# Two weight sums moved in VectorE's queue, four state copies given to ScalarE, one unit's scores moved up: a blocked attention followed by a bilinear feed-forward

## The chip, the cores and the metric

The kernel runs on one core of one Trainium2 chip. The metric is the time of one launch in device microseconds, as the median of several executions. A profile of one execution is at hand for each kernel. Engines in the profile: PE is TensorE's matmuls, PEld its weight loads, DVE is VectorE, ACT is ScalarE, POOL is GpSimd, SP is SyncE, which here issues transfers.

## The reference, cut to what matters

```python
# attention: 4 batches, 8 heads, 768 positions, 64 per head
intra = (qb @ kb^T * Dmask) @ vb             # within a block, decay lam^(i-j), lower triangle
inter = (qb * lam_pow) @ kv_state            # from the blocks before
out[block] = intra + inter
kv_state = lam_block * kv_state + (kb * rev_pow)^T @ vb
# feed-forward on x = attention output, 3072 x 512
a = x @ w_a ; b = x @ w_b                    # 512 x 1536 each
out = (a * b) @ w_out                        # 1536 x 512
```

## The kernel before

The work is cut into 24 units of 128 positions (six units make one sequence of a batch), and the units into seven groups. While TensorE does the feed-forward of one group, hooks at numbered slots insert the attention of later units. What goes where is a table, `PLAN`:

```python
ACT_COPY = (14, 16, 17, 18, 20, 21)          # units whose state copy is ScalarE's
FIRST_COPY = (15, 19)
PLAN = {
    0: [...(9, "P", 4), (9, "TW", 4), (9, "L", ...), (11, "P", 5), ...,
        (14, "T", 4), (17, "S", 4), (17, "P", 6), ..., (21, "V", 4), (22, "S", 5), (22, "LS", 9), ...,
        (29, "KS", 8), (30, "QS", 9), (33, "KS", 9), (33, "TW", 5)],
    1: [(0, "V", 6), (1, "S", 7), ...],
    2: [..., (11, "S", 10), (11, "S", 11), ..., (18, "S", 14), (19, "S", 15)],
    ...
```

P, KS and QS scale a unit's k and q by powers of lam. T transposes them on TensorE (later units are transposed by a transfer). S makes the scores of a unit and masks them. V adds to the state. L and LS issue loads. TW makes one of six *weight sums*. These serve the groups from the second on, whose feed-forward uses a scheme with seven products in place of eight and needs sums of weight blocks beforehand (the code is cut and simplified):

```python
def block_sums(t, b11, b21, b12, b22):       # four passes over 128 x 512 bf16
    nc.vector.tensor_sub(t[:, 0], b12, b11)
    nc.vector.tensor_sub(t[:, 1], b22, t[:, 0])
    nc.vector.tensor_sub(t[:, 2], b22, b12)
    nc.vector.tensor_sub(t[:, 3], b21, t[:, 1])

def piece_S(u):
    masks(u, scores(u))                      # scores: PSUM kq (TensorE); masks: m = kq * lotri (VectorE)

def kv_copy(u, ps, eng="dve"):               # state from PSUM to SBUF, its two diagonal blocks
    if eng == "act":
        for b in range(2):                   # two half copies
            nc.scalar.copy(st[p, :, b, :], ps[p, :, b, :])
    else:
        nc.vector.tensor_mul(st, ps, bdiag_bc)
```

The kernel uses seven PSUM banks in rotation. A matmul that needs a bank waits until its last reader is done (in the trace before, m_p waits 1.14 us for VectorE's mask). In the feed-forward of a group, m_q, m_r and m_p are the banks of the seven products; `c` and `ab` are sums and products made of them; `op` is the output product.

## Time and profile before

| | before |
|---|---|
| time, median of its first five runs | 220.97 us |
| span of the profiled run | 218.9 us |
| TensorE busy | 210.6 us, 96% |
| VectorE busy | 173.6 us, 79% |
| ScalarE busy | 106.8 us, 49% |

TensorE is nearly always busy, so the reading begins with its few waits and asks what stood in the other engine's queue at that moment. The prediction below shows those lines.

### The profile page before, as it was taken

The page shows a single profiled execution, that of the slowest core. Times are in us where ns is not written, and L with a number is a line of the kernel's source. Part 1 is how long each engine was busy: PE and PEld are TensorE (multiplying, and loading weights), DVE is VectorE, ACT ScalarE, POOL GpSimd, SP SyncE. Part 2 cuts the span into 40 slices and gives each one's busy share as a digit, 9 for nine tenths or more (in the row PEclk, how much of TensorE's full clock was granted, in tenths as well). Part 3 has the DMA queues.
Part 4 walks back from the last instruction along what each step waited for, and adds up shares of the span by engine and source line. Part 5 has one row for each costly group of instructions (what it writes and reads, how often), then busy time and mean ns, then how long its engine had stood idle before and what let it go on. Part 6 is the DMA issues. An engine that isn't in the chain of part 4 may idle for free.

```text
span 218.9 us, 5702 instructions
## 1 busy us (share of the span) xinstructions
PE 210.6 (96%) x2300; PEld 159.8 (73%) x2311; DVE 173.6 (79%) x309; ACT 106.8 (49%) x191; POOL 126.5 (58%) x143
## 2 busy tenths in 40 slices
PE   7799999999799999999999999999999999999994
PEld 2476444556787688865588887888987888989973
DVE  0992998956979488799968899879899787996860
ACT  3586223246771565613375636365546566443522
POOL 6879559974387279994079930599920156300330
PEclk9999999999999999999999999999999999999999
DMA  4999999999698959999999990399920500001302
GB/s 133 294 181 195 203 231 212 228 221 169 127 173 93 157 88 147 159 230 308 225 260 165 174 166 4 107 208 140 113 15 3 191 0 3 0 3 68 128 3 96
DMA packets 84686, 30.78 MB, mean 141 GB/s; under 512 B 71988, under 2 KB 81076, under 8 KB 84660
## 3 DMA queue, kind: packets, MB, share of 16 engines
q1 hardware_dynamic: 51668, 19.86, 45.2%
q0 software_dynamic: 32704, 10.49, 42.7%
q8 instruction: 18, 0.29, 0.5%
q10 hardware_dynamic: 288, 0.07, 0.1%
q14 instruction: 8, 0.07, 0.1%
HBM read 28.32 MB, written 6.29 MB: 158 GB/s over the span
## 4 chain that ended last, share of the span: by engine, by line
PE 56%; POOL 18%; DMA 13%; issue 5%; DVE 4%; SPq 2%; ACT 1%; POOLq 0%; DVEq 0%
PE m_q L565 18%; PE m_r L565 8%; PE op L802 7%; PE o_q L676 7%; POOL qk L277 5%; DMA wo_sb<-in_moe_w_out_dram 5%; PE m_p L565 4%; PE o_r L676 4%; POOL ab L612 4%; DMA kf<-in_k_dram 4%; PE o_ps L380 3%; POOL vb L299 3%; DMA k<-in_k_dram 3%; DMA qkf<-in_k_dram 2%; PE o_p L676 2%
## 5 line engine op out<-in xcount | busy, mean ns | idle before, releaser
L612 POOL TENSOR_TENSOR ab<-c,c 128x512 bf16<-128x512 bf16 x30 | 34.8, 1168 | 35.7 <-DVE c L610 35.4
L565 PEld LDWEIGHTS <-tw 128*128 128x128 bf16 x576 | 49.1, 98 | 6.1 <-issue 0.4
L565 PE MATMUL m_q<-xs,tw 128*128 128x256 bf16 (+1 forms) x288 | 36.1, 255 | 0.0
L802 PE MATMUL op<-wo_sb,ab 128*128 128x512 bf16 (+2 forms) x159 | 33.2, 347 | 0.7 <-issue 0.3
L361 DVE TENSOR_TENSOR m<-kq,lotri 128x512 bf16<-128x512 f32 x47 | 29.3, 680 | 0.1
L565 PEld LDWEIGHTS <-wa_sb 128*128 128x128 bf16 x288 | 24.7, 98 | 4.0 <-issue 1.3
L580 ACT COPY s<-m_q 128x512 f32<-128x512 f32 x30 | 17.6, 588 | 17.6 <-PE m_q L565 16.2
L619 DVE TENSOR_TENSOR ab<-c,m_q 128x512 bf16<-128x512 f32 x30 | 20.6, 686 | 6.7 <-PE m_q L565 4.4
L602 POOL TENSOR_TENSOR c<-s 128x512 bf16<-128x512 f32 x7 | 8.9, 1271 | 26.7 <-ACT s L580 26.7
L610 DVE TENSOR_TENSOR c<-u,m_r 128x512 f32<-128x512 f32 x30 | 20.4, 680 | 4.8 <-ACT u L580 4.8
L802 PEld LDWEIGHTS <-ab 128*128 128x128 bf16 x168 | 14.4, 98 | 12.3
L299 POOL DMA_DIRECT2D vb<-in_v_dram x24 | 22.3, 933 | 1.4 <-DMA wo_sb<-in_moe_w_out_dram 1.2
L599 DVE TENSOR_TENSOR c<-s,m_p 128x512 bf16<-128x512 f32 x23 | 15.8, 688 | 7.7 <-PE m_p L565 7.6
L616 DVE TENSOR_TENSOR c<-s,m_q 128x512 f32<-128x512 f32 x30 | 20.6, 685 | 0.5
L580 ACT COPY u<-m_q 128x512 f32<-128x512 f32 x30 | 17.8, 593 | 6.4 <-PE m_q L565 6.0
L580 ACT COPY s<-m_r 128x512 f32<-128x512 f32 x30 | 17.7, 590 | 6.4 <-PE m_r L565 6.4
L277 POOL TENSOR_TENSOR qk<-qf,lp_q 128x512 bf16<-128x512 f32 x18 | 18.8, 1044 | 1.2 <-DMA qf<-in_q_dram 1.2
L565 PE MATMUL m_p<-xT,wa_sb 128*128 128x256 bf16 (+1 forms) x144 | 18.1, 255 | 1.1 <-DVE m L361 1.1
L565 PE MATMUL m_q<-xT,tw 128*128 128x256 bf16 (+1 forms) x144 | 18.1, 255 | 0.3 <-DVE c L616 0.3
L403 ACT CAST xT<-o_ps 128x512 bf16<-128x512 f32 x22 | 11.9, 589 | 12.9 <-PE o_ps L380 12.5
L565 PE MATMUL m_q<-xT,wa_sb 128*128 128x256 bf16 (+1 forms) x144 | 18.1, 255 | 0.0
L565 PE MATMUL m_r<-xs,tw 128*128 128x256 bf16 (+1 forms) x144 | 18.1, 255 | 0.0
(118 smaller groups left out, 359.3 us busy)
## 6 DMA issues: line engine op xcount, KB each, us to landing
qf<-in_q_dram SPq DMA_DIRECT2D x14, 256.0 KB, 4.9
kf<-in_k_dram SPq DMA_DIRECT2D x14, 256.0 KB, 5.1
vb<-in_v_dram POOLq DMA_DIRECT2D x24, 128.0 KB, 5.5
out_dram<-o_two SPq DMA_DIRECT2D x6, 512.0 KB, 3.1
wa_sb<-in_moe_w_a_dram POOLq DMA_DIRECT2D x6, 256.0 KB, 6.2
wb_sb<-in_moe_w_b_dram POOLq DMA_DIRECT2D x6, 256.0 KB, 7.7
wo_sb<-in_moe_w_out_dram POOLq DMA_DIRECT2D x6, 256.0 KB, 8.1
out_dram<-o_kept SPq DMA_DIRECT2D x6, 256.0 KB, 5.5
```

Of the source, the lines that this page charges most:

```text
L277: eng_of(eng).tensor_mul(dst.rearrange("p (c b) d -> p b c d", b=2), x[:].rearrange("p (b c) d -> p b c d", b=2), lp.rearrange("p (b c) o ...
L299: nc.gpsimd.dma_start(out=vb, in_=vr[b, nb])
L361: nc.vector.tensor_mul(m, kq[i], lotri_bc)
L565: nc.tensor.matmul(ps[:, f, :], lhsT=w(k, f), rhs=x[:, k, :], start=(first and f == 0 and k == 0), stop=True, skip_group_check=True)
L580: nc.scalar.copy(t, ps)
L599: nc.vector.tensor_add(d["c11"], d["s12"][:, 0], p)
L610: nc.vector.tensor_add(c12, d["u2"], d["r"])
L612: nc.gpsimd.tensor_mul(ab[:, nf * i:nf * i + nf, 0:h], d["c11"], c12)
L616: nc.vector.tensor_add(d["c22"], d["s5"], d["q"])
L619: nc.vector.tensor_mul(ab[:, nf * i:nf * i + nf, h:2 * h], d["c22"], d["q"])
L676: nc.tensor.matmul(ps[:, t, :], lhsT=x(j, c)[:, t * BLK:(t + 1) * BLK], rhs=w(j)[:, c, :], start=(first and t == 0 and j == js[0] and c == ...
L802: nc.tensor.matmul(op[:, lo:hi], lhsT=ab[:, f, t * 128:(t + 1) * 128], rhs=wo_sb[:, f, lo:hi], start=(f == 0), stop=(f == FC - 1))
```

## The change

The intent: put the last two weight sums where VectorE is idle for a transfer, and take state copies off VectorE. The diff, cut to its lines:

```diff
-ACT_COPY = (14, 16, 17, 18, 20, 21)
-FIRST_COPY = (15, 19)
+ACT_COPY = (4, 10, 12, 13, 14, 16, 17, 18, 20, 21)
+FIRST_COPY = (11, 15, 19)
 ...
-        (9, "P", 4), (9, "TW", 4), (9, "L", ...
+        (9, "P", 4), (9, "L", ...
-        ... (22, "S", 5), (22, "LS", 9), (23, "P", 7), ...
+        ... (22, "S", 5), (22, "LS", 9), (22, "TW", 4), (23, "P", 7), ...
-        (30, "QS", 9), (33, "KS", 9), (33, "TW", 5)],
+        (30, "QS", 9), (31, "TW", 5), (33, "KS", 9)],
 ...
-    2: [..., (11, "S", 10), (11, "S", 11), ...
+    2: [..., (10, "S", 10), (11, "S", 11), ...
```

## The prediction

> **What bounds the kernel now.** I read the engine table first, then the list of who waited for whom on TensorE, then the order of time of TensorE and VectorE around each wait.
>
> ```profile
> PE 210.6 (96%) x2300; PEld 159.8 (73%) x2311; DVE 173.6 (79%) x309; ACT 106.8 (49%) x191; POOL 126.5 (58%) x143
> ...
> PEclk9999999999999999999999999999999999999999
> ```
>
> TensorE is busy in 210.6 of 218.9 us, at a granted clock that never drops. The change adds or removes no matmul, so it can only win part of the remaining 8.3 us. By five-microsecond stretches, 2.6 us of that gap lie in the first fifteen microseconds (1.26 + 1.01 + 0.36) and 3.15 us after 215 us (3.9 less 0.75 busy), under the last output; neither is touched. What is left is small and named by the list of waits:
>
> ```profile
> PE idle L213 <- DVE idle_sb L208: 1.3, 1, 1.3
> PE m_p L565 <- DVE m L361: 1.1, 1, 1.1
> ...
> PE kq L344 <- DVE ab L515: 0.3, 1, 0.3
> ...
> PE m_q L565 <- DVE c L616: 0.3, 1, 0.3
> ```
>
> Columns: who waited for whom, total us, times, longest. The first is the start-up. The other three all wait for VectorE, once each, and the change works exactly there. In order of time, TensorE (start, duration, work, idle before) around the three:
>
> ```profile
> 41.49 0.23 PE L344 MATMUL kq<-qkT 64*128 64x128 bf16 x1
> 42.04 0.38 PE L344 MATMUL kq<-qkT 64*128 64x128 bf16 x7 [0.32 <-DVE ab L515]
> 42.35 0.60 PE L802 MATMUL op<-wo_sb,ab 128*128 128x512 bf16 x2
> ...
> 57.82 0.61 PE L565 MATMUL m_r<-xs,tw 128*128 128x128 bf16 x8
> 59.57 0.61 PE L565 MATMUL m_p<-xT,wa_sb 128*128 128x128 bf16 x8 [1.14 <-DVE m L361]
> ...
> 60.46 0.61 PE L322 MATMUL tps<-ident,qk 128*128 128x128 bf16 x8
> 61.36 0.61 PE L565 MATMUL m_q<-xT,tw 128*128 128x128 bf16 x8 [0.29 <-DVE c L616]
> ```
>
> The reader should compare starts, not the idle figures[...]. An undisturbed set of eight scores takes 0.33 us from its start to the next (45.29 to 45.62 in the same view), a set of eight 128-column matmuls 0.45 (53.59 to 54.04), eight transposes 0.45 (42.79 to 43.24). So the three stalls cost 42.35 - 41.49 - 0.33 = 0.53 us, 59.57 - 57.82 - 0.45 = 1.30 us and 61.36 - 60.46 - 0.45 = 0.45 us. Sum: 2.28 us. That is the whole prize in reach.
>
> VectorE in the same stretch shows why:
>
> ```profile
> 37.51 1.82 DVE L277 TENSOR_TENSOR qk<-kf,lp_k 128x512 bf16<-128x512 f32 x1
> 39.25 0.41 DVE L518 TENSOR_TENSOR tw<-wb_sb,wa_sb 128x512 bf16<-128x512 bf16 x1
> ...
> 40.71 1.27 DVE L515 TENSOR_TENSOR ab<-a_sb,b_ps 128x512 bf16<-128x512 bf16 x2
> ...
> 55.10 0.69 DVE L277 TENSOR_TENSOR qk<-qkf,lp_k 128x512 bf16<-128x512 f32 x1 [2.28 <-DMA qkf<-in_k_dram]
> 55.71 0.42 DVE L518 TENSOR_TENSOR tw<-wb_sb,wa_sb 128x512 bf16<-128x512 bf16 x1
> 56.16 1.49 DVE L519 TENSOR_TENSOR tw<-wb_sb,tw 128x512 bf16<-128x512 bf16 x1
> ...
> 58.24 0.68 DVE L444 TENSOR_TENSOR st<-kvd,bdiag 128x512 bf16<-128x512 f32 x1
> 58.84 1.27 DVE L361 TENSOR_TENSOR m<-kq,lotri 128x512 bf16<-128x512 f32 x2
> ```
>
> Weight sum 4 sits ahead of the two products (ab) that free the banks the scores of unit 4 want. Weight sum 5 sits behind unit 9's k, which lands only at 55.10, and ahead of unit 7's masks; VectorE idles 2.28 us and then does the sums when TensorE needs the masks. From 76 us to 214 us the stretches leave TensorE idle for some 0.3 us in all, so nothing else of size is to be won.
>
> [...] the idle 2.28 us at 55.10 was not filled with the sums standing next in the queue. So position in program order is what the change buys. [...] eight transposes being shown as 0.61 us while the next work starts after 0.45, hence the starts above. [...] one weight-sum piece took 1.49 us instead of 0.42 while GpSimd ran a sum from 56.10 to 57.36, and k of unit 4 took 1.82 instead of 0.69 beside GpSimd's work from 37.69. [...] This is the main uncertainty for the new places of the sums.
>
> **The change part by part.** *Weight sum 4.* Its four pieces take from 39.25 to 40.71, 1.46 us. Without them the ab products, whose PSUM input is ready (no wait is shown before them), run at about 39.25 to 40.45, before the scores at 41.49: the 0.53 us go. In its new place, behind unit 5's masks, VectorE idles 2.00 us before unit 7's k, which waits for a transfer until 49.01. Masks of unit 5 ended at 47.01; with TensorE 0.53 us ahead and the state copy of unit 4 gone from the queue (0.60 us from start to start) they end near 46.4, so the sums fill 46.4 to 47.9. GpSimd's next scaling starts at 47.88; a collision would cost up to its 1.04 us, giving 48.9, still at the transfer's landing. Cost: 0 to 0.1 us.
>
> *Weight sum 5.* VectorE finishes unit 8's k at 52.8 and idles to 55.10. The sums take 1.46 us, to about 54.3; GpSimd's scaling of unit 9's q at 54.13 (1.04 us) may hold the last piece to 55.2. Then unit 9's k to 55.8, unit 6's state copy (it stays on VectorE) to 56.4, the first mask of unit 7 to 57.0, the second to 57.6. TensorE, 0.53 us ahead, wants the first bank at 57.82 + 0.45 - 0.53 = 57.74: no wait, 1.30 us go. The two sums behind the masks, 0.60 us each, end near 58.8; TensorE reaches the matmuls that waited for the second at 57.74 + 3 x 0.45 = 59.1: the 0.45 us go too, with 0.3 us to spare.
>
> *State copies of units 4, 10, 12, 13.* On VectorE one takes 0.68 us; on ScalarE it is two instructions of half the partitions:
>
> ```profile
> L442 ACT CAST st<-kvd x10: 364/367/370, 126.8 to 168.4; 64x256 bf16<-64x256 f32 x10
> ```
>
> ```profile
> L444 DVE TENSOR_TENSOR st<-kvd,bdiag x13: 677/682/692, 15.5 to 191.2; 128x512 bf16<-128x512 f32 x13
> ```
>
> That is 2 x 0.367 = 0.73 us each, 2.9 us in all on ScalarE, which is 49% busy, against 4 x 0.60 = 2.4 us of queue time off VectorE. ScalarE idles from 92.2 to 96.9 where unit 10's copy falls (its matmuls are at 93.41, its readers at 97.32), and between its output copies for 12 and 13. TensorE has no wait on VectorE there, so these three are worth 0 to 0.1 us. Unit 11 is the last block of its sequence and has no copy, so listing it with those copied first does nothing; the instruction order of the changed kernel confirms that.
>
> *Scores of unit 10 one place earlier.* TensorE's order changes only here. Its two masks (1.2 us) come before a c11 sum instead of after the last c22. That queue has about 0.45 us free in each period of 3.06 us, so the last c22 slips from 93.97 to about 94.7, against 94.94 where TensorE uses it: about 0.2 us to spare. Worth 0, with a small risk.
>
> Sum: 0.53 + 1.30 + 0.45 = 2.28, less an allowance of 0.1 to 0.2 for collisions: about 2.1 us, 1.0%. From 220.97 this gives 218.85 us.
>
> **The rivals.** *Transfers set the pace.* k of units 7 and 9 land at absolute times, and the loads of unit 10 were issued at 56.33 and 56.81, with a median landing of about 5 us; GpSimd would want them at 62.3 instead of 64.55. They land about 61.3 to 62.6, so GpSimd may wait some tenths, but it then has 1.13 us idle before its next product. Against it also: the transposes of units 8 and 9 have over 1 us of room. If it held, little of the 1.75 us after 57 us would survive: 220.2 to 220.6. [...] unit 7's or 9's k late: 0.3 to 1 us of the gain gone, 219.2 to 219.8. For it: the two collisions seen before; against it: 0.8 us of room at the first mask. *A new wait around 90 to 98 us* through unit 10's masks or ScalarE's copies: 0.2 to 0.6 us back, 219.1 to 219.5. Against it: ScalarE's idle there and the still free TensorE.
>
> **Range and chances.** The best case is 220.8 (the fastest run) less 2.3, or 218.5, less a tenth or two of luck; the likely spoilers leave 219.8. One of three runs before was 222.75, 0.8% off, so the medians can move a few tenths: range 218.1 to 219.9. Over 2% faster would need 4.4 us, more than all TensorE stalls between 15 and 214 us: 2%. Slower by over 2% would need a new chain of stalls of 4.4 us: 1%. Within 2%: 97%.
>
> **What would show it.** In the changed profile TensorE should be busy as before (210 us) with a span near 216.8; the waits on ab, m and c should be gone from its list or below 0.1; on VectorE the weight sums should stand in the former idle times before 49 and before 55 us, with those idle times down to about half a microsecond; the 70 us after 76 us should be a shifted copy. I am wrong if a wait of TensorE on VectorE of some 0.3 us or more remains between 50 and 62 us, if a wait appears at 90 to 98 us, or if the span falls by less than 1.5 us.

## The result, and the profile after

The changed kernel took 218.86 us (median of 5 runs, 218.78 to 219.09) against 220.97 (220.80 to 222.75). The ratio is 0.9889, with a 95% interval of 0.9851 to 0.9927. Ratios here are the mean time of one kernel's fast runs over that of the other's in the same rounds, so not quite the ratio of the medians.

The waits of TensorE after (who waited for whom, total us, times, longest); what is left besides these is 0.4, 0.3 and 0.2 us at the start and in gaps without a cause shown:

```profile
PE idle L213 <- DVE idle_sb L208: 1.3, 1, 1.3
PE tq L871 <- DVE scratch L864: 0.8, 3, 0.4
```

The three waits are gone. TensorE in order of time at the same three places (start, duration, work, count):

```profile
41.48 0.40 PE L344 MATMUL kq<-qkT 64*128 64x128 bf16 x8
41.81 0.60 PE L802 MATMUL op<-wo_sb,ab 128*128 128x512 bf16 x2
...
57.27 0.61 PE L565 MATMUL m_r<-xs,tw 128*128 128x128 bf16 x8
57.72 0.61 PE L565 MATMUL m_p<-xT,wa_sb 128*128 128x128 bf16 x8
...
58.62 0.61 PE L322 MATMUL tps<-ident,qk 128*128 128x128 bf16 x8
59.10 0.61 PE L565 MATMUL m_q<-xT,tw 128*128 128x128 bf16 x8
```

Each next start follows after 0.33, 0.45 and 0.48 us. Against the same instructions before, TensorE is ahead by 42.35 - 41.81 = 0.54 us at the first, 59.57 - 57.72 = 1.85 us at the second, and 61.36 - 59.10 = 2.26 us at the third.

VectorE shows how (the last bracket is the idle time before an instruction and what ended it):

```profile
46.38 0.42 DVE L518 TENSOR_TENSOR tw<-wb_sb,wa_sb 128x512 bf16<-128x512 bf16 x1
...
49.25 0.69 DVE L277 TENSOR_TENSOR qk<-kf,lp_k 128x512 bf16<-128x512 f32 x1 [1.33 <-DMA kf<-in_k_dram]
...
52.93 0.42 DVE L518 TENSOR_TENSOR tw<-wb_sb,wa_sb 128x512 bf16<-128x512 bf16 x1
...
55.36 0.69 DVE L277 TENSOR_TENSOR qk<-qkf,lp_k 128x512 bf16<-128x512 f32 x1 [0.89 <-DMA qkf<-in_k_dram]
55.97 0.68 DVE L444 TENSOR_TENSOR st<-kvd,bdiag 128x512 bf16<-128x512 f32 x1
56.57 1.28 DVE L361 TENSOR_TENSOR m<-kq,lotri 128x512 bf16<-128x512 f32 x2
```

Both sums now stand in front of a transfer that VectorE has to wait for anyway; their pieces take 0.42 to 0.43 us each, so none was held up beside GpSimd's work. The idle times that remain are 1.33 and 0.89 us. In sum TensorE's busy time is nearly as before (210.2 of 217.1 us), VectorE's is 169.9 us (3.7 less) and ScalarE's 109.4 (2.6 more).

The lead does not stay at 2.26. It falls twice. The first place is the scores of units 10 and 11 (kq). Before, in one stretch of TensorE:

```profile
92.33 0.60 PE L565 MATMUL m_q<-xs,tw 128*128 128x256 bf16 x4
92.86 0.62 PE L344 MATMUL kq<-qkT 64*128 64x128 bf16 x16
93.41 0.40 PE L411 MATMUL kvd<-vb,qk 128*128 128x128 bf16 x4
```

and after, where unit 10 has moved:

```profile
87.45 0.60 PE L565 MATMUL m_q<-xs,tw 128*128 128x256 bf16 x4
87.98 0.40 PE L344 MATMUL kq<-qkT 64*128 64x128 bf16 x8
88.31 0.61 PE L565 MATMUL m_r<-xs,tw 128*128 128x256 bf16 x4
```

Four matmuls of 256 columns take 0.44 us from their start to the next where they stand among their own kind (88.76 to 89.20 for m_p in the same view), but 0.53 us where scores of tile 64\*128 follow (92.33 to 92.86): 0.09 us are lost on the way in. Sixteen scores together take 0.55 us (92.86 to 93.41) and eight 0.33 (87.98 to 88.31), so eight more cost 0.22, and by this difference 0.11 us are a fixed part of each set. The split pays both once more: 0.09 + 0.33 + 0.33 - 0.55 = 0.20 us. (64\*128 and the like is the tile that the profile shows with a matmul.) In the trace before, sixteen scores take the same 0.55 us where matmuls of tile 64\*64 follow (96.77 to 97.32). In that trace the new weights are loaded only together with the first matmul of the new tile: the loads start at 92.86, after 0.21 us without one, and at 97.32, and so do the matmuls. Where the tile stays the same, the first load for the m_q at 92.33 starts at 92.22, 0.11 us before it. From the m_q at 89.71 (before) and 87.45 (after), a lead of 2.26, it falls to 93.41 - 91.37 = 2.04 us at the state's matmuls.

The second place is ScalarE at the start of the fifth group. Before:

```profile
141.80 0.62 ACT L580 COPY s<-m_p 128x512 f32<-128x512 f32 x1
142.28 0.63 ACT L580 COPY u<-m_q 128x512 f32<-128x512 f32 x1
```

After:

```profile
139.77 0.62 ACT L580 COPY s<-m_p 128x512 f32<-128x512 f32 x1
140.44 0.58 ACT L580 COPY u<-m_q 128x512 f32<-128x512 f32 x1
```

The copy u starts 0.48 us after its forerunner before and 0.67 us after. TensorE's next addition to that bank comes 0.14 us later for it: the lead falls from 142.41 - 140.38 = 2.03 to 142.96 - 141.07 = 1.89 us. It stays there: 212.08 - 210.20 = 1.88 us at the last output product, against 1.8 us by the spans, 218.9 and 217.1.

So this pair of profiled runs differs by 1.85 us in time (220.64 and 218.79), and the medians by 2.11. The profiled run before was faster than all five executions that the median is taken from.

### The profile page after: what moved, and what is told of

The parts are those of the page before. It is cut to its first block, busy times and chain, and to the rows that moved or that the text cites.

```text
span 217.1 us, 5705 instructions
## 1 busy us (share of the span) xinstructions
PE 210.2 (97%) x2300; PEld 159.6 (74%) x2311; DVE 169.9 (78%) x305; ACT 109.4 (50%) x199; POOL 126.8 (58%) x143
## 4 chain that ended last, share of the span: by engine, by line
PE 92%; DMA 3%; ACT 2%; SPq 1%; issue 1%; DVE 0%; ACTq 0%
PE m_q L565 24%; PE op L802 14%; PE m_r L565 12%; PE o_q L676 7%; PE m_p L565 6%; PE o_ps L380 5%; PE b_ps L488 5%; PE a_ps L488 5%; PE o_r L676 4%; PE kq L344 3%; DMA k<-in_k_dram 3%; PE o_p L676 2%; PE kvd L411 1%; SPq L229 1%; PE tps L322 1%
```

## The experiments

Twelve runs in three batches, all correct; the last four ran on another chip than the first eight. Each batch shares its runs of the kernel before, 11 of them: medians 221.05, 221.08 and 220.79 us. Times below are medians of six executions unless it is said otherwise; two of these medians hold one slow execution, which is said there. The intervals of the ratios are 0.003 to 0.005 wide on either side, so differences of 0.2 us between two kernels are read from the traces, where the distance between two starts on TensorE repeats to a few hundredths (eight scores from 104 to 107 us: 0.32 to 0.33 us in the trace after and in four of the experiments; the start-up shifts all of them: the feed-forward begins at 17.37 to 18.03 us in the fourteen traces).

### Weight sum 4 alone

```diff
-        (9, "P", 4), (9, "TW", 4), (9, "L", ...
+        (9, "P", 4), (9, "L", ...
-        (22, "LS", 9), (23, "P", 7)
+        (22, "LS", 9), (22, "TW", 4), (23, "P", 7)
```

> Kernel before with weight sum 4 moved, nothing else. Theory (unit 9's k lands at a fixed time, so VectorE's queue behind it does not move): TensorE's 0.53 us at the scores of unit 4 go, but the wait before m_p grows from 1.14 to about 1.67 us in the list of waits, since the masks of unit 7 still end after unit 9's k and weight sum 5; time unchanged, ratio 1.000 within 0.001. Rival (the stalls add up independently): the wait before m_p stays 1.14 us, time 0.53 us less, ratio 0.9976.

Measured: 220.88 us against 221.05, ratio 0.9996 (0.9960 to 1.0032): no gain to be seen, as the theory has it, but the interval still holds the rival's 0.9976. The trace decides. The wait at the scores of unit 4 is gone from the list, and the other one has grown, in the profiled run to twice its size, more than expected because unit 9's k also landed later (VectorE took it up at 56.05 instead of 55.10):

```profile
PE m_p L565 <- DVE m L361: 2.3, 1, 2.3
```

```profile
59.86 1.28 DVE L361 TENSOR_TENSOR m<-kq,lotri 128x512 bf16<-128x512 f32 x2
```

m_p starts 0.73 us after the first mask of unit 7 begins, here (60.59) as before (59.57 after 58.84) and with the copies alone (59.71 after 58.98), although TensorE reached this wait 0.16 us earlier than before in this trace and 0.04 us earlier with the copies alone. So VectorE's queue sets that start, and what TensorE wins ahead of it is lost there.

This run took 222.88 us, and its mean granted clock was 0.992. The windows show where (start and end, then width, busy time and count of PE, PEld, DVE, ACT and POOL, the granted clock of TensorE, the transfers' share and GB/s):

```profile
60.00:61.00 1.00, 0.41 (x8) 0.41 (x8) 1.00 (x2) 0.00 (x0) 0.00 (x0) 1.00 1.29 233
61.00:62.00 1.00, 1.00 (x15) 1.00 (x13) 1.00 (x3) 0.59 (x2) 0.12 (x1) 0.58 1.29 217
62.00:63.00 1.00, 1.00 (x12) 1.00 (x11) 0.33 (x1) 0.73 (x2) 1.00 (x2) 0.50 1.33 223
63.00:64.00 1.00, 1.00 (x13) 1.00 (x11) 0.29 (x1) 0.86 (x1) 1.00 (x2) 0.50 1.32 219
64.00:65.00 1.00, 1.00 (x15) 1.00 (x14) 0.77 (x2) 0.00 (x0) 0.27 (x1) 0.71 1.34 217
```

After the 2.32 us wait the granted clock fell to 0.50 (62 to 64 us). The clock lost in the four windows from 61 us is 0.42 + 0.50 + 0.50 + 0.29 = 1.71 us, so 3.4 us at half clock: here the wait cost time again after it had ended. Two of the six runs had the clock 0.992 (222.29 and 222.88 us); the other four lie at 220.63 to 220.98.

### Weight sum 5 alone

```diff
-        (30, "QS", 9), (33, "KS", 9), (33, "TW", 5)],
+        (30, "QS", 9), (31, "TW", 5), (33, "KS", 9)],
```

> Kernel before with weight sum 5 moved ahead of unit 9's k, nothing else. Theory: both waits of TensorE near 58 to 61 us go (1.30 + 0.45 us by starts), the wait at the scores of unit 4 (0.32 us shown, 0.53 by starts) stays; time 1.75 us less, 219.2 us, ratio 0.992. Rival (the state copies are needed as well to make room on VectorE): 0.3 us or more of wait remains after 57 us, ratio 0.994 or above.

Measured: 219.00 us, ratio 0.9919 (0.9880 to 0.9958). TensorE starts m_p at 58.27 (59.57 before) and the m_q that waited at 59.61 (61.36): ahead by 1.30 and 1.75 us, to the hundredth as expected. No wait on VectorE after 57 us is left, with every state copy of the four where it was. The lead stays at 1.75 us up to the last matmuls, so here neither of the two later losses occurs.

### The state copies alone

```diff
-ACT_COPY = (14, 16, 17, 18, 20, 21)
+ACT_COPY = (4, 10, 12, 13, 14, 16, 17, 18, 20, 21)
```

> Kernel before with the state copies of units 4, 10, 12, 13 by ScalarE, nothing else. Theory: VectorE's 2.4 us of queue time are not where TensorE waits; the three waits of TensorE stay within 0.05 us of those before, time within 0.1 us, ratio 1.000. Rival (VectorE's load as such is what bounds, 79% busy): 0.5 us or more off.

Measured: 221.42 us (221.14 without the one execution, 224.28 us at a clock of 0.992, that counts as slow), ratio 1.0015 (0.9978 to 1.0052): no gain. In detail the expectation missed. TensorE came 0.18 us later from the start-up, so the wait at unit 4's scores was shorter by that, and VectorE took up unit 9's k 0.25 us later and began the first mask of unit 7 0.14 us later (58.98), so the wait for that mask was 1.3 us. What matters is the end of the trace: the copy u at the start of the fifth group starts late here too, and TensorE falls back by 0.16 us there (from 0.14 to 0.30 behind the kernel before).

### Both weight sums, no copies, scores of unit 10 in place

The diffs of the first two experiments together.

> Kernel before with both weight sums moved; state copies and scores of unit 10 as before. Theory: all three waits go, 2.28 us by starts, and nothing is lost near 90 us: 218.7 us, ratio 0.9897, up to 0.2 us under the changed kernel. Rival (the copies matter): slower than the changed kernel by 0.2 us or more, with a wait on masks of unit 5 or on a weight sum left.

Measured: 218.67 us (218.66 without the slow execution), ratio 0.9887 (0.9857 to 0.9916), as expected, and not slower than the changed kernel. So by the times the two moves alone give the whole gain. The profiled run of this kernel is the one that counts as slow (221.71 us, at a clock of 0.998), so its trace is no measure of the time. It shows what still can go wrong. Its start-up was 0.6 us longer, VectorE took up unit 8's k only at 54.69 (52.32 in the trace after) and unit 9's at 57.62 (55.36), and two pieces of work were stretched beside GpSimd, which scaled unit 9's q from 56.37 to 57.42 and made a sum from 57.39 to 58.82:

```profile
56.43 1.27 DVE L521 TENSOR_TENSOR tw<-wa_sb,tw 128x512 bf16<-128x512 bf16 x1
57.62 1.75 DVE L277 TENSOR_TENSOR qk<-qkf,lp_k 128x512 bf16<-128x512 f32 x1
```

So late transfers and collisions can still bring a wait back: TensorE waited 2.10 us for the mask there, and the clock stayed at 1.00 in the windows after it, read to 63 us.

### The changed kernel again

> The changed kernel once more, as the yardstick of the three below on the same chip: 218.86 us within 0.2, ratio 0.989. The gap of 0.27 us that its first trace shows on TensorE before a matmul of the fourth group (start 141.07) is an accident of that run if it is not there again; if it is there, the change brought it.

Measured: 218.91 us, ratio 0.9900 (0.9851 to 0.9949). The gap is there again: the copy u starts 0.67 us after its forerunner, at 140.39, and the lead falls by 0.16 us. So it is no accident. (The expectation counts the groups from zero; its fourth is the fifth here.) Over all fourteen traces, the six with the four copies on ScalarE show it (0.65 to 0.67 us), the copies alone among them, and the eight without (0.47 to 0.48) do not. Which of the four copies brings it is not shown. In the traces before and after alike ScalarE's queue shows two semaphore events at the copies' line (142.1 to 142.3 us before, 140.1 to 140.5 after). Before, the copy starts ahead of the shown end of its forerunner (142.28 against 142.42), after the change only behind it (140.44 against 140.38); why is not shown by any run.

### Scores of unit 10 put back

```diff
-    2: [..., (10, "S", 10), (11, "S", 11), ...
+    2: [..., (11, "S", 10), (11, "S", 11), ...
```

(on the changed kernel; an island is a set of scores of tile 64\*128 between matmuls of tile 128\*128)

> Changed kernel with the scores of unit 10 put back beside those of unit 11. Theory ([...] the move makes two such islands of one): TensorE 0.2 us ahead of the changed kernel from there on, time about 0.2 us less, 218.65 us. Rival (the move gives VectorE's masks time that is needed): a wait of TensorE on a mask or a sum of 0.1 us or more appears between 88 and 97 us, time same or longer.

Measured: 218.74 us, ratio 0.9883 (0.9841 to 0.9926), against 218.91 of the changed kernel in the same rounds. The totals do not separate the two; the trace does. TensorE is 0.14 us behind the changed kernel ahead of that place, by its start-up, and 0.07 us ahead from the state's matmuls on (91.30 against 91.37): 0.21 us won at that place, and no wait appears between 88 and 97 us.

### Scores of units 14 and 15 joined, early

```diff
-    (18, "S", 14), (19, "S", 15)
+    (18, "S", 14), (18, "S", 15)
```

(on the kernel of the experiment above)

> As the run with unit 10's scores put back, and the scores of unit 15 joined to those of unit 14 one place earlier. Theory: one more island less, another 0.18 us, 218.45 us, 0.4 us under the changed kernel. Rival (four score banks at once leave too few for the next group's first matmuls): a wait of TensorE on a mask appears near 106 us and eats it.

Measured: 219.42 us, ratio 0.9900 (0.9858 to 0.9941). Both theories were wrong. The banks sufficed, but unit 15's q and k, which a transfer transposes, were not there yet:

```profile
105.56 0.40 PE L344 MATMUL kq<-qkT 64*128 64x128 bf16 x8 [0.97 <-DMA qkT<-qk]
```

### Scores of units 14 and 15 joined, late

```diff
-    (18, "S", 14), (19, "S", 15)
+    (19, "S", 14), (19, "S", 15)
```

(on the kernel with unit 10's scores put back)

> Changed kernel with unit 10's scores put back beside unit 11's, and unit 14's scores moved one place later, beside unit 15's (the run that joined them one place earlier waited 0.97 us for unit 15's transposing transfer). Theory (each pair of switches between 64-row and 128-row matmuls costs about 0.2 us): no wait on a transfer, TensorE gains 0.2 us at 106 us on top of the 0.2 us at 88 us, about 218.55 us, the fastest of all. Rival: the four masks behind each other delay the next group, a wait of 0.1 us or more near 107 us, no gain over 218.74.

Measured: 218.58 us (four runs, 218.37 to 218.71), ratio 0.9883 (0.9840 to 0.9927), against 220.79 in the same rounds. No wait on a transfer or a mask. From the output product to the next group's first matmul TensorE takes 105.89 - 101.58 = 4.31 us, where the changed kernel takes 106.28 - 101.75 = 4.53: 0.22 us won again. By the traces this kernel is ahead of the changed one by 0.4 us at 106 us. Its time is the lowest median of all, but it ran in other rounds and on another chip than the changed kernel, and the two ratios overlap, so that it beats it by time is not shown.

### Joined late, without the copies

The diffs of both weight sums and of the late joining, on the kernel before.

> Kernel before with both weight sums moved and unit 14's scores joined to unit 15's, the state copies all as before. Theory: with the copy of unit 13 still in VectorE's queue ahead of four masks, the first c12 sum of group 3 comes about 0.5 us later than without; if TensorE waits for it, this is where the copies on ScalarE earn something: 0.2 to 0.5 us slower than the kernel with the copies moved. Rival (no wait there): the same 218.5 us.

Measured: 218.94 us, ratio 0.9898 (0.9860 to 0.9937). TensorE has no wait near the joined scores: the first c12 sum of the next group comes 2.79 us after the group's first matmul in this trace (109.78 - 106.99) and 2.80 us with the copies on ScalarE (108.69 - 105.89). The rival holds: unit 13's copy earns nothing there. The 218.94 are another matter: in the profiled run (219.31 us) VectorE took up unit 9's k at 56.47, over one microsecond later than in the trace of the changed kernel (0.65 us of it are start-up: 18.03 against 17.38), and 0.3 us of the wait for a c sum came back.

### The collision with GpSimd's sum

```diff
-SUM_ON_VEC = {1: (2,), ...
+SUM_ON_VEC = {1: (0, 2), ...
```

(on the kernel before: one sum of group 1 from GpSimd to VectorE)

> Kernel before, with the first c11 sum of group 1 on VectorE (0.6 us more work in its queue ahead of unit 7's masks) and so no GpSimd sum beside weight sum 5. Theory [...]: weight sum 5 takes 1.46 us, the first mask ends about 0.45 us earlier in spite of the added work, TensorE's wait before m_p is about 0.7 us instead of 1.14, time 0.4 to 0.5 us less, ratio 0.998. Rival (only the order counts, and the long piece was no collision): the piece stays at 1.49 us, the wait grows by 0.6 us, time 0.6 us more.

Measured: 220.67 us against 221.08, ratio 0.9957 (0.9917 to 0.9998). The piece that took 1.49 us takes 0.42:

```profile
56.27 0.42 DVE L519 TENSOR_TENSOR tw<-wb_sb,tw 128x512 bf16<-128x512 bf16 x1
```

The first mask of unit 7 begins at 58.48 instead of 58.84 although a 0.6 us sum now stands before it. TensorE wins 0.35 us at m_p and no more later (this execution started 0.12 us later; the medians give 0.41 us, as expected), and its wait now sits one product earlier (0.6 us, before m_r, for the sum that was moved). GpSimd's sum beside the piece was thus behind a good part of the wait, 0.35 us of it by this trace.

### A longer wait

```diff
         block_sums(t, wa_sb[:, 0:2, c], ...)
+        for _ in range(2 if i == 5 else 0):
+            nc.vector.tensor_sub(t[:, 3], wa_sb[:, 2:4, c], t[:, 1])
```

(on the kernel before; the repeated work writes the same values)

> Kernel before with two of weight sum 5's pieces of work done again, 0.68 us more ahead of unit 7's masks. TensorE's wait before m_p grows from 1.14 to about 1.8 us. Theory [...]: time 0.7 us more, about 221.7, clock 1.000 in most runs. Rival (any lengthening adds clock loss in proportion): clock near 0.995 and 1.2 us more or above.

Measured: 222.60 us, ratio 1.0062 (1.0020 to 1.0103). The six runs fall in two kinds: 221.58, 221.82 and 222.50 us at a clock of 0.998 to 1.000, and 222.71, 222.83 and 223.57 at 0.992. The profiled run is of the second kind, with a wait of 2.5 us rather than 1.8, for VectorE took up unit 9's k at 55.81, 0.7 us later than in the trace before. The theory's "most runs" was not met; but the clock was either low or not, with nothing between, which a loss in proportion would not give. The wait of 2.10 us in the slow run without the copies left the clock at 1.00 in the windows to 63 us; those of 2.32 us (weight sum 4 alone) and 2.52 us (here) were followed by 0.50. That the wait stayed near the planned 1.8 us in the half without the loss, and that a late landing as in the profiled run lengthened it in the other, is the author's estimate; of the runs without the loss none was profiled.

### A long wait

The same with `range(5 ...)`.

> The same with five more pieces, 1.7 us more: TensorE's wait before m_p about 2.8 us. Theory [...]: clock 0.992 in nearly all runs and time 1.7 + 1.1 = 2.8 us more, about 223.8 us. Rival (the low clock of single runs is an accident that lengthens the wait, not its result): clock 1.000 in most runs and 222.7 us.

Measured: 224.64 us (five runs), ratio 1.0151 (1.0105 to 1.0198); the clock was 0.991 or 0.992 in all five. The wait in the profiled run was 3.3 us, and the clock was low from 63.7 us (0.85 in the window from 63 us, 0.50 in the next two), 1.2 us after the wait's end at 62.51. The theory holds: the low clock comes with the long wait in all five runs, and in the profiled one it follows it. In the trace above the clock lost in the windows from 62 to 66 us is 0.35 + 0.50 + 0.50 + 0.35 = 1.70 us, so 3.4 us at half clock, as with weight sum 4 alone (1.71 and 3.4); here the windows to 66 us show 0.15 + 0.50 + 0.50 = 1.15 us, with the clock still at 0.50, and the mean clock over the span gives an estimate of 223.2 x (1 - 0.992) = 1.8 us. Whether the place of a wait counts beside its length (2.32, 2.52 and 3.32 us with the loss, 2.10 us without), no run shows. The time was 0.8 us above its figure; half a microsecond of this is the wait, longer than meant, the rest was not followed up.

## Why the prediction was right

The time was right to 0.01 us; the sum under it was right in its main terms and wrong in two small ones.

**The three stalls.** Predicted by starts 0.53, 1.30 and 0.45 us, measured as steps of the lead 0.54, 1.31 and 0.41. The order was the reason, as said: each sum now fills idle time in front of a transfer.

**That they add up.** The prediction summed them. The run with weight sum 4 alone shows that they only do so together: without the second move the 0.53 us are handed on to the wait for unit 7's mask, since VectorE's queue there starts from a transfer. With both, 2.26 us. That a change without fewer matmuls "can only win part of the remaining 8.3 us" of idle time did no harm here, but it is no bound: the 0.2 us of each set of scores stand inside TensorE's busy time.

**The allowance for collisions, 0.1 to 0.2 us.** Not needed for the sums: all eight pieces took 0.42 to 0.43 us in the trace after. So it was in seven of the eight traces with weight sum 5 moved; in the eighth, the slow run of the kernel without the copies, one piece took 1.27 us and unit 9's k 1.75, so there the allowance would have been too small. The idle times left over, 1.33 and 0.89 us, are larger than the half microsecond that I expected, because no collision used them up and the transfers too came 0.25 us later than in the trace before. By the records k of unit 4 (1.82 us from 37.51) had started before GpSimd's work (37.69), and again after the change (2.24 us from 37.49, GpSimd from 38.09): in both traces the one that started first took longer than the 0.69 us of unit 9's k.

**State copies, "worth 0 to 0.1 us".** Wrong in sign: with the two sums in place they earned nothing (218.67 us without them, 218.74 with them and unit 10's scores put back, in other rounds), and all kernels that have them lose some 0.14 to 0.16 us at one ScalarE copy of the fifth group. I had looked only at idle time near the copies.

**Scores of unit 10, "Worth 0, with a small risk".** Wrong in size: about 0.2 us lost, not by the late c22 sum that I feared (no wait appears there) but on TensorE itself, by changing to the scores' tile and back once more (0.21 us won back where unit 10's scores were put back). So the time after 76 us was not quite the shifted copy that was forecast; of the signs of being wrong none appeared.

Together the traces give 2.26 - 0.22 - 0.14 = 1.90 us rather than 2.1. The medians give 2.11. The difference lies in the executions of the kernel before: the profiled one is 0.33 us faster than their median. That the others had a longer wait for unit 9's k is likely, but none of them was profiled. Of its 33 runs beside the experiments four had a clock of 0.992 and took 222.79 to 223.44 us; of 45 runs of kernels with weight sum 5 moved (the changed one among them) none had it. That these four runs had a wait as long as the profiled ones with the loss (2.32 us and more) is inferred from the two experiments with longer waits; none of them was profiled. So the exactness of the figure is in part luck: two losses that I had not seen, an allowance that was not needed, and a median before that lay above the trace which the sum was read from.

**The rivals.** The one with transfers setting the pace was right about its mechanism in the run of weight sum 4 alone, and in runs in which k of unit 9 comes late. In the two traces of the changed kernel it did not bind. The one in which k of unit 7 or 9 comes late beside GpSimd's work came true only in that slow run (unit 9's k took 1.75 us). The new wait at 90 to 98 us did not appear, though ScalarE's copies did cost something, at 141 us. The span, predicted near 216.8, was 217.1.

## What to carry to other kernels

When an engine idles for a transfer with later work of its queue behind it (here VectorE for 2.28 us, with the sums next in line), move work that nobody waits for in front of that wait; and check which of several stalls on the main engine share one source, since removing one of them may only lengthen the next. Before taking a group of small matmuls apart for scheduling reasons, price the change of tile shape on TensorE, here 0.20 to 0.22 us for each further island of them between larger matmuls, in three pairs of traces. A rare slow run can be the main engine's clock falling after a stall that a late transfer has stretched: with weight sum 4 moved alone the clock was 0.50 after a wait of 2.32 us, with unit 9's k taken up 0.95 us late, and with the stall removed, a mean clock of 0.992 was not seen in 45 runs. Single late runs stayed (219.99, 220.54, 221.27 and 221.71 us), and in the one of them that was profiled the transfers came late.
